# Dense blocks of 128 rows instead of 256 in a fused top-k attention and squared-ReLU network

## The chip, the cores and the metric

The kernel runs on one core of a Trainium2 chip. The metric is the device time of one execution in microseconds (us); lower is better. The core's engines work side by side, each through its own list of instructions in order: TensorE (PE; its weight loads are PEld), VectorE (DVE), ScalarE (ACT), GpSimd (POOL), and SyncE (SP), which here issues the DMAs.

## The reference

For 8 batches and 8 heads of 576 queries and keys of 64 numbers, each query keeps its 32 highest scores; the softmax runs over these alone. The result, 4608 tokens of 512 numbers, goes through a dense network of width 2048.

```python
scores = scale * np.matmul(q, k.transpose(0, 1, 3, 2))
kth = np.partition(scores, -top_k, axis=-1)[..., -top_k:-top_k + 1]
scores = np.where(scores >= kth, scores, -1000000000.0)
scores = scores - np.max(scores, axis=-1, keepdims=True)
attn = np.exp(scores)
attn = attn / (np.sum(attn, axis=-1, keepdims=True) + 1e-09)
x = np.matmul(attn, v)            # as [4608, 512] tokens
...
h = np.maximum(x @ w_in, 0.0)     # w_in 512 x 2048
out = h * h @ w_out               # w_out 2048 x 512
```

## The kernel before

**Steps.** The attention runs in 144 steps, counted by `u` from 0. A step takes two groups of 128 query rows (two heads of one chunk; a batch has four chunks of 128 rows and a rest of 64). The steps are software-pipelined: while step u finds the top 32 of its rows, PE computes the scores of step u + 3 (`scores`, L213) and ACT copies them out of the accumulation banks (L219); DVE prepares step u + 2 (`split`, L251 or L253 to L256, and `join`, L263); ACT and POOL make the weights of step u - 1 (`below` L354, `expo` L363, `mask` L359); SP turns them by a DMA transpose (`turn`, L402); PE multiplies them with the values (`products`, L429); and ACT puts the divided result into a chunk of tokens, `x_tok` (`place`, L457). Steps 0 to 124 are one loop (L702), 125 to 141 a second one (L798), in which the dense work that is left is taken faster; the last two are written out.

**Top 32.** Per step DVE does four rounds of MAX8 (L302) with three MATCH_REPLACE8 between them (L306), on candidates that `split` and `join` have sorted: maxima and minima of the halves and quarters of a row. The minima are POOL's: it adds (L278) and subtracts the maxima (L270) as whole numbers.

**Who takes the maxima.** `split` has two ways. It "lends" when POOL has room: one DVE operation of 576 columns (L251), and `bring` (L235), a PE product with the unit matrix, hands a part of the result back into the bank that `join` reads. Otherwise DVE does three operations of 288 columns (L253, L254, L256) and POOL gets less. A step that lends may also be "joint": then `join` does one operation of 288 columns on DVE (L263) and POOL one more (L270 of 288), otherwise DVE does two. `bring` waits for ACT's copies of the next scores, and `join` waits for `bring`.

**The ledger.** The order is fixed when the program is written. `debt` counts the work owed by POOL ("G") and ACT ("A"); each step takes off 5.76 and 6.0, and `owe` adds what is issued. `split` lends outside the last steps only while the debt of POOL is under 4.9 (L239), and is joint while it is under 3.68 at first, from step 125 on 4.28.

**Dense work.** When a chunk of `x_tok` is full, `x_unit` (L474) turns it by DMA (L497) into `xT`. After the second chunk of a pair, and three steps later (two near the end), `block` (L519) opens a block of 256 rows. It has 8 "ups" and 8 "downs". An up is a piece for PE: two of the 16 slices of w_in, each with 4 matmuls of 256 columns (L531), into a bank of 512 columns. ACT takes the ReLU of it (L537), and the square is ACT's (L542) or POOL's (L545), by the ledger; up to step 18 and in the last ones it is always POOL's. A down is 4 matmuls with w_out (L559); after four downs ACT copies the rows out (L566) and SP stores them. The rests of 64 rows of two batches, and the last batch's chunks, make blocks of 128 rows already, with 4 ups of 4 slices. `dense` (L591) gives PE two pieces a step, an up and a down in turn if both are there, in the loop's two places, before `bring` and at the step's end; without work it issues idle matmuls (`idle_piece`, L575).

**Buffers.** `h2` holds the hidden rows, 3 buffers of 256 rows; the raw weights land in the same buffers (`weight_units`, L606), 16 loads from step 1 on, one a step, and 16 casts by ACT or POOL from step 4 on, one a step (L785).

Of the kernel before, what the change touches and what calls it, by code (L numbers as in the profile page):

```python
# [14 lines left out]
bf16 = mybir.dt.bfloat16  # L15
# [7 lines left out]
def kernel(  # L23
# [10 lines left out]
    B, H, S, D = q.shape  # L34
# [8 lines left out]
    KH, NF = 4, d_ff // 128  # L43
# [12 lines left out]
    now = [0]  # L56
# [139 lines left out]
    Z, DEEP = U - 19, 9  # L196
# [271 lines left out]

    moves, ups, downs = [], [], []
    ripe = {}  # L470
    xts = {}


    def x_unit(now, b, c):  # L474
        last = b == B - 1
        cs = (c,) if last else (c - c % 2, c - c % 2 + 1)
        if c == cs[0]:
            xts[b, cs] = ffp.tile([128, len(cs), KH, 128], bf16, name=f"xT_{len(cs)}", bufs=2)
        xt = xts[b, cs]
        to = xt[:, c - cs[0]]  # L480

        def done():
            if c == cs[-1]:
                stores = [[(slice(0, 128), out[b * S:b * S + 512].rearrange("(p c) d -> p c d", c=4)[:, z])] for z in cs]
                block(lambda kh: xt[:, :, kh, :], stores)

        def by_tensor(now):
            tp = ps_one.tile([128, KH, 128], bf16, name="gen", bufs=2)
            for kh in range(KH):
                pin(nc.tensor.transpose(tp[:, kh, :], x_tok[b, c][:, kh * 128:(kh + 1) * 128], id_h[:, :]))  # L490
            pin(nc.scalar.activation(to, tp[:, :, :], AF.Copy))
            done()

        if last:
            moves.append(by_tensor)
        else:
            pin(nc.sync.dma_start_transpose(out=to, in_=x_tok[b, c][:, :]))  # L497
            ripe.setdefault(now + (3 if now < Z - 8 else 2), []).append(done)

    def rem_unit(now, b):  # L500
        owe(A=0.3)
# [17 lines left out]
    def block(xt, stores):  # L519
# [4 lines left out]
        def up(f0):  # L524
            def go():
                if f0 == 0:
                    held["h2"] = ffp.tile([128, NF, 256], bf16, name="h2", bufs=3)
                hp = ps_one.tile([128, 512], f32, name="gen", bufs=2)[:, :]
                for n in range(per):
                    for kh in range(KH):  # L530
                        pin(nc.tensor.matmul(out=hp[:, n * n_rows:(n + 1) * n_rows], lhsT=w_in[:, kh, (f0 + n) * 128:(f0 + n + 1) * 128],  # L531
                                             rhs=xt(kh), start=(kh == 0), stop=(kh == KH - 1)))
                h2 = held["h2"][:, f0:f0 + per, 0:n_rows]

                def bend():
                    rl = ffp.tile([128, 512], f32, name="rl", bufs=4)
                    pin(nc.scalar.activation(rl[:, :], hp, AF.Relu))  # L537
                    owe(A=0.5)
                    flat = rl[:, :].rearrange("p (n r) -> p n r", n=per)
                    if DEEP + 9 < now[0] < U - 7 and debt["A"] < 6.0 and debt["G"] > 3.6:  # L540
                        owe(A=0.62)
                        later.append(lambda: pin(nc.scalar.activation(h2, flat, AF.Square)))  # L542
                        return
                    owe(G=1.05)
                    squares.append(lambda by: pin(by.tensor_mul(h2, flat, flat)))  # L545
                    if not hold["squares"]:
                        square()
                late.append(bend)
                if f0 + per == NF:
                    downs.extend(down(c, p) for c in range(len(stores)) for p in range(4))  # L550
            return go
# [54 lines left out]
    def weight_units():  # L606
        loads, casts = [], []
        for dst, src in ((w_in, moe_w_in.rearrange("(kh p) n -> p kh n", p=128)), (w_out, moe_w_out.rearrange("(kh p) n -> p kh n", p=128))):
            to, width = dst[:, :, :], src.shape[2]
            for g in range(8):  # L610
                if width >= 1024:
                    at = (slice(None), g // 2, slice((g % 2) * 1024, (g % 2) * 1024 + 1024))
                else:
                    at = (slice(None), slice(2 * g, 2 * g + 2), slice(None))
                box = {}

                def load(src=src, at=at, box=box):
                    t = ffp.tile([128, NF, 256], bf16, name="h2", bufs=3)
                    t = t[:, :, :].rearrange("p f r -> p (f r)")[:, 0:2048].bitcast(f32)
                    box["t"] = t if not isinstance(at[1], slice) else t.rearrange("p (a n) -> p a n", a=2)  # L620
                    pin(nc.sync.dma_start(out=box["t"], in_=src[at]))

                def cast(dst=dst, at=at, box=box):
                    if debt["A"] > debt["G"]:
                        owe(G=1.25)
                        pin(nc.gpsimd.tensor_copy(dst[at], box["t"]))
                    else:
                        owe(A=0.95)
                        pin(nc.scalar.activation(dst[at], box["t"], AF.Copy))
                loads.append(load)  # L630
                casts.append(cast)
# [70 lines left out]
    for u in range(Z):  # L702
# [79 lines left out]
        if 1 < u < 24 and not ups and not downs:  # L782
            idle_piece(2)
        turn_x(u)
        if w_casts and u >= 4:  # L785
            w_casts.pop(0)()
        if w_loads and u >= 1:
            w_loads.pop(0)()
# [75 lines left out]
    u = U - 2  # L864
# [36 lines left out]
        square()  # L901
    empty(two)

    xl = ffp.tile([128, KH, 128], bf16, name="xT_1", bufs=2)
    hl = ffp.tile([128, NF, 256], bf16, name="h2", bufs=3)

    def x_last(khs):
        tp = ps_one.tile([128, KH, 128], bf16, name="gen", bufs=2)
# [219 lines left out]
```

## Time and profile before

| | before |
|---|---|
| median of 3 runs | 843.42 us (843.41 to 844.8) |
| the profiled execution | 843.64 us |
| its span, first to last instruction | 841.8 us |
| DVE busy | 816.4 us, 97% |
| ACT busy | 791.5 us, 94% |
| POOL busy | 785.0 us, 93% |
| PE busy, matmuls | 710.4 us, 84% |
| chain that ended last | DVE 53%, issue 15%, POOL 13%, ACT 11%, PE 7% |

The busy times are unions of the instructions' times on one engine; the chain goes back from the last instruction to what released each. A step takes some 5.4 to 5.5 us. All numbers of the trace are of this one execution, so a sum is made against 843.64 us.

### The profile page before, as it was taken

Reading aid. Unit: us, or ns where it says so; the run is one execution under the profiler, and the core shown is the slowest. Engines: PE = TensorE matmul, PEld = TensorE weight load, DVE = VectorE, ACT = ScalarE, POOL = GpSimd, SP = SyncE. Lnnn points to the kernel's source line nnn. Section 1 sums busy time; section 2 is a strip of 40 time slices with the busy share of each in tenths; the row PEclk is TensorE's granted clock in tenths of the full one; section 3 lists DMA queues with packets and bytes.
Section 4 is the critical chain, followed back from the end, with each engine's and each line's share of the span. In section 5 each row is a group of like instructions: output and inputs, shape, how many; then the busy total and the mean of one; then the engine's idle time right before and its main releaser. Section 6 shows DMA issues by size and latency. Waiting matters only on the chain.

```text
span 841.8 us, 19913 instructions
## 1 busy us (share of the span) xinstructions
PE 710.4 (84%) x6061; PEld 446.6 (53%) x6062; DVE 816.4 (97%) x3411; ACT 791.5 (94%) x1513; POOL 785.0 (93%) x638
## 2 busy tenths in 40 slices
PE   8898987788888879788788888788888888989986
PEld 4554545455545545455555554455555554656554
DVE  5999999999999999999999999999999999999995
ACT  4897999999999999999999999999999999999983
POOL 3788999999999999999999999999999999999771
PEclk9999999999999999999999999999999999999999
DMA  4796786654546556445565455555566557433442
GB/s 112 163 216 158 193 178 112 111 118 101 118 105 104 117 111 130 97 103 109 114 124 110 104 111 124 124 111 109 118 104 124 118 104 152 79 76 64 94 84 55
DMA packets 300883, 98.06 MB, mean 116 GB/s; under 512 B 284768, under 2 KB 293216, under 8 KB 300768
## 3 DMA queue, kind: packets, MB, share of 16 engines
q1 hardware_dynamic: 299424, 96.28, 56.1%
q8 instruction: 50, 0.82, 0.4%
q14 instruction: 65, 0.53, 0.2%
q10 hardware_dynamic: 1344, 0.43, 0.2%
HBM read 36.70 MB, written 9.44 MB: 55 GB/s over the span
## 4 chain that ended last, share of the span: by engine, by line
DVE 53%; issue 15%; POOL 13%; ACT 11%; PE 7%; DVEq 0%; ACTq 0%; POOLq 0%
DVE m L302 23%; DVE cat L306 15%; DVE s L251 7%; POOL cat L270 7%; DVE cat L263 5%; POOL cat L278 5%; ACT s L219 3%; ACT h L542 2%; PE sc_b L235 2%; ACT rl L537 1%; ACT marks_b L354 1%; ACT marks_a L354 1%; ACT w_two_a L363 1%; PE sc_b L213 1%; PE dn_ps L578 1%
## 5 line engine op out<-in xcount | busy, mean ns | idle before, releaser
L302 DVE MAX8 m<-cat 128x8 f32<-128x100 f32 (+3 forms) x1152 | 428.7, 414 | 0.2
L278 POOL TENSOR_TENSOR cat<-s 128x864 int32<-128x864 int32 (+2 forms) x144 | 265.0, 1840 | 5.9 <-DVE cat L263 3.5
L306 DVE MATCH_REPLACE8 cat<-m,cat 128x100 f32<-128x100 f32 (+2 forms) x864 | 252.7, 300 | 0.1
L270 POOL TENSOR_TENSOR cat<-cat,s 128x576 int32<-128x576 int32 (+1 forms) x144 | 196.3, 1363 | 3.3 <-DVE s L251 1.8
L213 PE MATMUL sc_b<-qkT 64*128 64x288 f32 (+1 forms) x640 | 117.4, 447 | 55.3 <-DVE cat L263 49.2
L235 PE MATMUL sc_b<-s,id_f 128*128 128x144 f32 x536 | 98.3, 306 | 57.4 <-ACT s L219 56.5
L559 PE MATMUL dn_ps<-w_out,h 128*128 128x512 bf16 x560 | 143.9, 382 | 1.3 <-POOL h L545 0.7
L531 PE MATMUL gen<-xT,w_in 128*128 128x256 bf16 (+1 forms) x1088 | 128.6, 263 | 1.9 <-ACT rl L537 1.1
L235 PEld LDWEIGHTS sc_b<-s,id_f 128*128 128x128 f32 x536 | 75.0, 190 | 101.0 <-ACT s L219 97.4
L531 PEld LDWEIGHTS <-w_in 128*128 128x128 bf16 x1344 | 110.2, 98 | 32.3 <-issue 19.7
L354 ACT ACTIVATE marks_a<-s,m 128x576 bf16<-128x576 f32 x144 | 124.2, 871 | 0.4 <-POOL w_two_c L359 0.2
L354 ACT ACTIVATE marks_b<-s,m 128x576 bf16<-128x576 f32 x142 | 118.5, 847 | 0.0
L219 ACT ACTIVATE s<-sc_b 128x576 f32<-128x576 f32 x144 | 103.7, 720 | 15.5 <-PE sc_b L213 8.2
L213 PE MATMUL sc_a<-qkT 64*128 64x288 f32 (+1 forms) x640 | 111.5, 430 | 0.4 <-DVE s L251 0.3
L219 ACT ACTIVATE s<-sc_a 128x576 f32<-128x576 f32 x144 | 104.8, 728 | 5.5 <-PE sc_a L213 3.7
L251 DVE TENSOR_TENSOR s<-sc_a,s 128x576 f32<-128x576 f32 x134 | 100.2, 748 | 0.0
L537 ACT ACTIVATE rl<-gen 128x512 f32<-128x512 f32 x140 | 96.3, 692 | 0.5 <-PE gen L531 0.5
L213 PEld LDWEIGHTS sc_b<-qkT 64*128 64x128 f32 (+1 forms) x640 | 47.6, 175 | 85.5 <-DVE cat L263 64.9
L270 POOL TENSOR_TENSOR cat<-cat 128x288 int32<-128x288 int32 x113 | 89.2, 789 | 0.9 <-DVE shares L434 0.9
L542 ACT ACTIVATE h<-rl 128x512 bf16<-128x512 f32 x123 | 89.2, 729 | 0.0
L559 PEld LDWEIGHTS <-h 128*128 128x128 bf16 x560 | 47.8, 98 | 68.4 <-issue 31.9
L263 DVE TENSOR_TENSOR cat<-sc_b,s 128x288 f32<-128x288 f32 x175 | 75.0, 444 | 5.8 <-PE sc_b L235 5.8
(137 smaller groups left out, 1190.5 us busy)
## 6 DMA issues: line engine op xcount, KB each, us to landing
v_raw<-in_v_dram SPq DMA_DIRECT2D x31, 256.0 KB, 3.1
out_dram<-wide SPq DMA_DIRECT2D x31, 256.0 KB, 2.9
q_raw<-in_q_dram SPq DMA_DIRECT2D x30, 256.0 KB, 3.6
k_raw<-in_k_dram SPq DMA_DIRECT2D x30, 256.0 KB, 3.6
h<-in_moe_w_in_dram SPq DMA_DIRECT2D x8, 512.0 KB, 5.1
h<-in_moe_w_out_dram SPq DMA_DIRECT2D x8, 512.0 KB, 4.7
q_raw<-in_q_dram SPq DMA_DIRECT2D x32, 32.0 KB, 3.1
v_raw<-in_v_dram SPq DMA_DIRECT2D x32, 32.0 KB, 2.7
```

The lines of the kernel that those rows point to most:

```text
L213: pin(nc.tensor.matmul(out=sc[j][r if rest else slice(0, 128), x, 0:HALF], lhsT=qkT[r, 0, c * 128:min(S, (c + 1) * 128)], rhs=qkT[r, 1, j ...
L219: pin(nc.scalar.activation(s[:, :, j, :], sc[j][:, :, 0:HALF], AF.Copy))
L235: pin(nc.tensor.matmul(out=far[:, x, :], lhsT=id_f[:, :], rhs=st[w]["tops"][:, x, 1, :], start=True, stop=True))
L251: pin(tt(tops, *quarters, op=ALU.max))
L263: pin(nc.vector.tensor_tensor(d["cat"][:, :, lo:lo + QUAR], far, d["tops"][:, :, 0, :], op=op))
L270: pin(nc.gpsimd.tensor_tensor(at, at, top, op=ALU.subtract))
L278: pin(nc.gpsimd.tensor_tensor(cat[:, :, QUAR + lo:QUAR + hi], both[:, :, 0, lo:hi], both[:, :, 1, lo:hi], op=ALU.add))
L302: pin(nc.vector.max(out=m[r][:, x, :], in_=cat[:, x, at]))
L306: pin(nc.vector.match_replace(out=cat[:, x, at], in_to_replace=m[r][:, x, :], in_values=cat[:, x, at], imm_value=NEG))
L354: pin(nc.scalar.activation(pairwise(marks[u % 2][:, x, :]), d["s"][:, x], AF.Relu, bias=d["m"][3][:, x, 7:8], scale=-1.0))
L531: pin(nc.tensor.matmul(out=hp[:, n * n_rows:(n + 1) * n_rows], lhsT=w_in[:, kh, (f0 + n) * 128:(f0 + n + 1) * 128], rhs=xt(kh), start=(kh ...
L559: pin(nc.tensor.matmul(out=op[:, :], lhsT=held["h2"][:, f, c * 128:(c + 1) * 128], rhs=w_out[:, f, :], start=(f == 0), stop=(f == NF - 1)))
```

## The change

Every chunk that is turned gets a block of its own, of 128 rows: 28 blocks of 4 ups and 4 downs in place of 14 of 8 and 8. An up of such a block has 4 slices with 4 matmuls of 128 columns. `h2` becomes 5 buffers of 128 rows, `xT` 4 buffers of one chunk. Up to step 20 a block opens two steps after its turn, not three, and the casts of the weights start in step 3.

```diff
--- before.py
+++ after.py
@@ -468,21 +468,14 @@
 
     moves, ups, downs = [], [], []
     ripe = {}
-    xts = {}
 
 
     def x_unit(now, b, c):
         last = b == B - 1
-        cs = (c,) if last else (c - c % 2, c - c % 2 + 1)
-        if c == cs[0]:
-            xts[b, cs] = ffp.tile([128, len(cs), KH, 128], bf16, name=f"xT_{len(cs)}", bufs=2)
-        xt = xts[b, cs]
-        to = xt[:, c - cs[0]]
+        to = ffp.tile([128, KH, 128], bf16, name="xT", bufs=4)
 
         def done():
-            if c == cs[-1]:
-                stores = [[(slice(0, 128), out[b * S:b * S + 512].rearrange("(p c) d -> p c d", c=4)[:, z])] for z in cs]
-                block(lambda kh: xt[:, :, kh, :], stores)
+            block(lambda kh: to[:, kh, :], [[(slice(0, 128), out[b * S:b * S + 512].rearrange("(p c) d -> p c d", c=4)[:, c])]])
 
         def by_tensor(now):
             tp = ps_one.tile([128, KH, 128], bf16, name="gen", bufs=2)
@@ -495,7 +488,7 @@
             moves.append(by_tensor)
         else:
             pin(nc.sync.dma_start_transpose(out=to, in_=x_tok[b, c][:, :]))
-            ripe.setdefault(now + (3 if now < Z - 8 else 2), []).append(done)
+            ripe.setdefault(now + (3 if 20 < now < Z - 8 else 2), []).append(done)
 
     def rem_unit(now, b):
         owe(A=0.3)
@@ -524,7 +517,7 @@
         def up(f0):
             def go():
                 if f0 == 0:
-                    held["h2"] = ffp.tile([128, NF, 256], bf16, name="h2", bufs=3)
+                    held["h2"] = ffp.tile([128, NF, 128], bf16, name="h2", bufs=5)
                 hp = ps_one.tile([128, 512], f32, name="gen", bufs=2)[:, :]
                 for n in range(per):
                     for kh in range(KH):
@@ -615,7 +608,7 @@
                 box = {}
 
                 def load(src=src, at=at, box=box):
-                    t = ffp.tile([128, NF, 256], bf16, name="h2", bufs=3)
+                    t = ffp.tile([128, NF, 128], bf16, name="h2", bufs=5)
                     t = t[:, :, :].rearrange("p f r -> p (f r)")[:, 0:2048].bitcast(f32)
                     box["t"] = t if not isinstance(at[1], slice) else t.rearrange("p (a n) -> p a n", a=2)
                     pin(nc.sync.dma_start(out=box["t"], in_=src[at]))
@@ -782,7 +775,7 @@
         if 1 < u < 24 and not ups and not downs:
             idle_piece(2)
         turn_x(u)
-        if w_casts and u >= 4:
+        if w_casts and u >= 3:
             w_casts.pop(0)()
         if w_loads and u >= 1:
             w_loads.pop(0)()
@@ -901,8 +894,8 @@
         square()
     empty(two)
 
-    xl = ffp.tile([128, KH, 128], bf16, name="xT_1", bufs=2)
-    hl = ffp.tile([128, NF, 256], bf16, name="h2", bufs=3)
+    xl = ffp.tile([128, KH, 128], bf16, name="xT", bufs=4)
+    hl = ffp.tile([128, NF, 128], bf16, name="h2", bufs=5)
 
     def x_last(khs):
         tp = ps_one.tile([128, KH, 128], bf16, name="gen", bufs=2)
```

The ledger sees the blocks at other times, so the order of the program moves. The first place is DVE where step 15 begins: the last join of step 14 (L263), then the split for step 17, and the first round of step 15. Before:

```order
L263 TENSOR_TENSOR cat<-sc_b,s 128x2x144
L251 TENSOR_TENSOR s<-sc_a,s 128x4x144
L302 MAX m<-cat 128x8 x2
L306 MATCH_REPLACE cat<-m,cat 128x100 x2
L440 RECIPROCAL shares<-av_ps 128x4
```

and with the change:

```order
L263 TENSOR_TENSOR cat<-sc_b,s 128x2x144
L253 TENSOR_TENSOR sc_b<-sc_a,s 128x2x144
L254 TENSOR_TENSOR s<-sc_a,s 128x2x144
L256 TENSOR_TENSOR cat<-sc_a,s 128x2x144
L302 MAX m<-cat 128x8 x2
L306 MATCH_REPLACE cat<-m,cat 128x100 x2
L440 RECIPROCAL shares<-av_ps 128x4
```

Step 15 no longer lends: three operations stand for one, and at its end two joins for one. Over the program that is 133 steps with L251 in place of 134, 11 with L253 to L256 in place of 10, and 176 joins in place of 175. Which steps are joint also shifts (15, 16, 17, 19 and 21 are not, before 20 to 23).

The second place is ACT in step 124, between the copies of the scores of this step and of the next (`rl` is a ReLU's result, `h2` a square, `w_two` the exponentials, `marks` the masks, `qkT` a head's turned queries). Before:

```order
L457 ACTIVATE x_tok_8932<-av_ps_121,shares_120 128x64 x2
L354 ACTIVATE marks_b_118<-s_9400,m_8449 128x576
L345 ACTIVATE low_9740<-neg_9738 128x1
L363 ACTIVATE w_two_a_103<-s_9400,low_9666 128x2x576
L363 ACTIVATE w_two_b_104<-s_9482,low_9740 128x2x576
L146 ACTIVATE qkT_9701<-gen_9772 128x512
L354 ACTIVATE marks_a_117<-s_9482,m_8449 128x576 x2
L457 ACTIVATE x_tok_9009<-av_ps_121,shares_120 128x64 x4
```

and with the change (L530 is the ReLU, L535 the square there):

```order
L457 ACTIVATE x_tok_9656<-av_ps_121,shares_120 128x64 x2
L354 ACTIVATE marks_b_118<-s_10177,m_9117 128x576
L345 ACTIVATE low_10546<-neg_10544 128x1
L530 ACTIVATE rl_10555<-gen_10520 128x512
L363 ACTIVATE w_two_a_103<-s_10177,low_10448 128x2x576
L535 ACTIVATE h2_10378<-rl_10555 128x512
L363 ACTIVATE w_two_b_104<-s_10266,low_10546 128x2x576
L530 ACTIVATE rl_10590<-gen_10572 128x512
L146 ACTIVATE qkT_10495<-gen_10597 128x512
L354 ACTIVATE marks_a_117<-s_10266,m_9117 128x576
L535 ACTIVATE h2_10378<-rl_10590 128x512
```

Two ReLUs and two squares have come into this step. In steps 119 to 121 ACT gets one ReLU and one square less, in steps 125 to 135 two ReLUs less; from the copies of step 119 to those of step 136 it is the same number of ReLUs (24) and output copies (6), and 21 squares for 20. Over the whole program ACT has the same number of each, and the squares on POOL stay 17, six of them now before step 24 in place of three. Idle matmuls of 512 columns on `dn_ps` go from 203 to 165. SP's DMAs keep their number and kinds.

## Rows read from the trace of the kernel before

**Rows 1.** Busy time by stretch, 200 to 700 us (stretch, length, busy us of each engine, instructions).

```profile
200.00:700.00 500.00, 417.21 (x3592) 266.64 (x3590) 497.40 (x2084) 493.03 (x947) 500.00 (x385) 1.00 0.56 114
```

**Rows 2.** DVE's waits, first from 80 to 718 us, then from 718 to 786.

```profile
DVE cat L306 <- POOL cat L270: 1.1, 5, 0.3
DVE cat L263 <- PE sc_b L235: 0.8, 3, 0.4
...
DVE cat L263 <- PE sc_b L235: 4.0, 6, 1.1
```

**Rows 3.** PE's waits from 718 to 786 us.

```profile
PE sc_b L235 <- ACT s L219: 3.7, 5, 1.4
```

**Rows 4.** Busy time by stretch: step 14, steps 126 to 136, steps 137 to 141.

```profile
95.17:100.58 5.41, 5.23 (x38) 2.73 (x36) 5.41 (x24) 5.41 (x10) 5.41 (x5) 1.00 0.77 208
...
718.35:785.10 66.75, 61.13 (x579) 41.26 (x580) 62.60 (x269) 66.75 (x137) 65.48 (x52) 1.00 0.39 75
785.10:816.03 30.93, 26.71 (x250) 15.66 (x248) 30.75 (x133) 27.39 (x55) 21.09 (x22) 1.00 0.44 91
```

**Rows 5.** Pieces on PE in order of time (start, us); then the loads of w_in.

```profile
764.47 1.05 PE L531 MATMUL gen<-xT,w_in 128*128 128x256 bf16 x8
765.35 1.03 PE L559 MATMUL dn_ps<-w_out,h 128*128 128x512 bf16 x4
...
771.00 1.06 PE L531 MATMUL gen<-xT,w_in 128*128 128x128 bf16 x16
771.90 1.03 PE L559 MATMUL dn_ps<-w_out,h 128*128 128x512 bf16 x4
...
L531 PEld LDWEIGHTS <-w_in 128*128 128x128 bf16 x1344 | 110.2, 98 | 32.3 <-issue 19.7 <-PE sc_b L213 0.4
```

**Rows 6.** DVE's groups, shapes apart (busy us, mean ns of one).

```profile
L251 DVE TENSOR_TENSOR s<-sc_a,s 128x576 f32<-128x576 f32 x134 | 100.2, 748 | 0.0
...
L253 DVE TENSOR_TENSOR sc_b<-sc_a,s 128x288 f32<-128x288 f32 x10 | 4.7, 465 | 2.0 <-ACT s L219 1.6
...
L256 DVE TENSOR_TENSOR cat<-sc_a,s 128x288 f32<-128x288 f32 x10 | 4.5, 448 | 0.0
```

**Rows 7.** POOL's groups, shapes apart.

```profile
L278 POOL TENSOR_TENSOR cat<-s 128x864 int32<-128x864 int32 x113 | 227.6, 2014 | 0.0
L270 POOL TENSOR_TENSOR cat<-cat,s 128x576 int32<-128x576 int32 x134 | 188.3, 1405 | 2.6 <-DVE s L251 1.8
L270 POOL TENSOR_TENSOR cat<-cat 128x288 int32<-128x288 int32 x113 | 89.2, 789 | 0.9 <-DVE shares L434 0.9
...
L545 POOL TENSOR_TENSOR h<-rl 128x512 bf16<-128x512 f32 x17 | 17.6, 1044 | 0.2 <-ACT rl L537 0.2
L278 POOL TENSOR_TENSOR cat<-s 128x288 int32<-128x288 int32 x10 | 7.9, 794 | 5.9 <-DVE cat L263 3.5 <-ACT s L219 2.4
```

**Rows 8.** SP's first chunk turn; DMA issues with us to landing.

```profile
92.21 1.38 SPq L497 DMA_TRANSPOSE xT<-x_tok  x1
...
h<-in_moe_w_in_dram SPq DMA_DIRECT2D x8, 512.0 KB, 5.1
...
xT<-x_tok SPq DMA_TRANSPOSE x28, 2.7
```

**Rows 9.** ACT in order of time in steps 126 and 127 (start, us).

```profile
723.86 0.66 ACT L537 ACTIVATE rl<-gen 128x512 f32<-128x512 f32 x1
724.34 0.85 ACT L354 ACTIVATE marks_a<-s,m 128x576 bf16<-128x576 f32 x1
725.00 0.70 ACT L542 ACTIVATE h<-rl 128x512 bf16<-128x512 f32 x1
725.52 0.84 ACT L354 ACTIVATE marks_a<-s,m 128x576 bf16<-128x576 f32 x1
```

**Rows 10.** Busy time by stretch, 68 to 74 us; PE's granted clock stands third from the right.

```profile
68.00:70.00 2.00, 0.25 (x2) 0.25 (x4) 2.00 (x5) 0.47 (x1) 1.46 (x2) 1.00 1.10 358
...
72.00:74.00 2.00, 1.94 (x7) 1.02 (x7) 1.00 (x4) 2.00 (x4) 2.00 (x2) 0.51 0.42 79
```

## The prediction

> **What bounds the kernel now.** I read the busy time by stretches first, since an average over the program hides which engine ends the waits where. From 200 to 700 us VectorE (DVE) is busy 497.4 of 500 us, GpSimd (POOL) all 500.0, ScalarE (ACT) 493.0 and TensorE (PE) 417.2 [rows 1]. The reader is to see three engines with next to no idle time. In that part a change can only add or take work on DVE or POOL; a better order of dense pieces on PE has no idle time of DVE to win back.
>
> Next come DVE's own waits. From 80 to 718 us it waits 1.1 us on POOL's second halves (L270) and 0.8 us on `bring`, the PE product that hands the borrowed maxima back (L235) [rows 2]. From 718 to 786 us it waits 4.0 us, in six waits, always on `bring` [rows 2]. Who makes `bring` late stands in PE's waits of that stretch: 3.7 us on ACT's copies of the scores (L219) [rows 3]. And the stretch 718.35 to 785.10 (steps 126 to 136) shows why: ACT is busy 66.75 of 66.75 us while DVE reaches 62.60 [rows 4]. So the last part before the end is bound by ACT, the long middle by DVE and POOL together. After 785.10 DVE is busy 30.75 of 30.93 us, ACT has 3.5 us and POOL 9.8 us to spare [rows 4].
>
> **The change, part by part.** The sum is made against the profiled execution: 843.64 us, 841.8 of it span, 1.84 around it. That is 0.22 above the median of the three runs shown, 843.42. A measurement of this kernel tells about 0.2% from no change, 1.7 us.
>
> *TensorE.* 14 blocks of 256 rows become 28 of 128. Relus, squares, output copies and down products keep their number; only the up products are cut otherwise: a piece of 8 matmuls of 256 columns becomes one of 16 of 128. The kernel before has both. The piece of eight starts at 764.47 and the next piece 0.88 us later; the piece of sixteen starts at 771.00 and its successor 0.90 us later [rows 5]. 112 pieces at 0.02 make 2.2 us of PE, spread over 128 steps, and 38 idle matmuls fewer take more than that away. PE has 83 us free between 200 and 700 [rows 1]. Cost 0; without that cover it would be 2.2 us.
>
> *DVE in step 15.* The first block now starts in step 14 and not 19. Its four squares are sent to POOL, which in the program's ledger pushes POOL's debt over the limit when step 15 splits its scores. So one step no longer borrows POOL: three operations of 288 columns (465, 448 and 448 ns) take the place of one of 576 (748), and one more join is done, of the shape that takes 448 [rows 6]: 1.36 - 0.75 + 0.45 = 1.06 us. DVE has no idle time there: in the window that starts with step 14 it is busy 5.41 of 5.41 us [rows 4]. This term is the surest of all, +1.06.
>
> *POOL in the same steps.* Three squares more at 1044 ns, +3.13. The step that doesn't borrow, and doesn't join on POOL, swaps 2014 + 1405 + 789 for twice 794 (the two kinds of 288 columns cost the same), -2.62 [rows 7]. Net +0.51. POOL has no gap from 200 to 700, and DVE's waits on it (1.1 us) show that it sets the pace by the end of the middle [rows 1, 2]. Where POOL sets the pace, DVE's 1.06 us come out of DVE's waits and only POOL's 0.51 stay; where it doesn't, 1.06 stay. I take 0.8 for both terms together.
>
> *Weight loads and chunk turns.* Five landing buffers for three, casts a step sooner. A load now has two steps, some 11 us, before its cast; w_in takes 5.1 us to land [rows 8]. Loads, turns and casts keep their number and their order on SP. Nothing, then; were the cover gone, a cast would hold ACT or POOL for the rest of a landing, at most 5.1 us once. The early chunks get two steps, not three, from turn to use: the first turn is issued at 92.21 and lands some 2.7 us later, 94.9, and step 14, which uses it, begins at 95.17 [rows 4, 8]. The cover is thin but there; if a turn came 1 us late, PE would stand 1 us before `bring`. The four buffers for the turned chunks hold as much as two pairs did, and five hidden blocks of 128 rows are more than the two or three that are open at once.
>
> *ACT in the middle.* Before, two chunks arrive at once, so some steps have two ups and some none; now most have one. The bursts make ACT's copies late, which is the 0.8 us wait on `bring` [rows 2]. I take half of it back: -0.4, with 0 and -0.8 as bounds.
>
> *ACT in the tail.* Here the order of work decides. Between the score copies of step 124 and of step 125 ACT gets two relus and two squares that were not there. From one start to the next a relu takes 0.48 and a square 0.52 us [rows 9]: 2.0 us more. In the three steps before, it gets one relu and one square less, 1.0 us. From step 125 to 136 two relus fewer, -0.96. Over the whole stretch, from the copies of step 119 to those of step 136, that is one square more, +0.52. ACT is the bound, so lateness there is DVE's wait. If the lead of 1.0 us is lost because ACT catches up with DVE in between, the peak is +2.0. If smoother steps let every copy come in time, the waits of 4.0 us go. I take +0.5, nearest to the count, with -4.0 and +2.0 as ends. After step 136 four ups fall into one step, where ACT has room [rows 4]: 0.
>
> Sum: 843.64 + 0.8 - 0.4 + 0.5 = 844.54 for a profiled execution, 844.3 against the median; I say **844.4 us**.
>
> **Rivals.** *Slower: ACT's backlog is carried to the end.* Place: step 124, with two ups where there were none. Price: the whole 2.0 us in the tail, 1.06 in the head, nothing back in the middle: 843.6 + 3.1 = 846.7. For it: ACT has no gap from 718 to 785, so nothing is recovered there. Against: its work in these steps is nearly the same in total. It decides if ACT is already level with DVE when step 124 begins.
>
> *Faster: even steps end the waits of the tail.* The 4.0 us on `bring` and the 0.8 go, 1.06 is paid: 843.6 - 3.7 = 839.9. For it: all these waits follow steps with two or three ups. Against: the tail has just as many relus, and 100% of ACT is not a burst.
>
> *PE's clock falls in sparse steps.* Steps 16, 17 and 29 to 31 have one piece and two idle matmuls now. PE is busy 0.25 of the two us before 70; from 72 to 74 the granted clock is 0.51, the lower of its two levels, 1.2 GHz, and DVE stands still 1.0 us of the two [rows 10]. Two such places: 843.6 + 0.8 + 2 = 846.4. Against: from 80 to 718 us DVE waits on `bring` only three times [rows 2], so it mostly comes early enough to be slowed a little.
>
> *The narrow pieces are bound by their weight loads.* A load of w_in has a mean of 98 ns [rows 5]. If a 128-column matmul had to wait for its whole load, a piece of sixteen would take 1.57 us, 0.69 more than the 0.88. Some 16 pieces in steps 126 to 136 would add 11 us to a PE that has 5.6 free there [rows 4], so DVE would be 5.4 later: some 849. Against it: the piece of sixteen that did take 0.90 [rows 5], 56 ns a matmul, so loads run under the matmuls. The Trainium skill (TensorE: Matmul & The Clock Gate, section "Back-to-back issue gap") says that a real stream of load and matmul keeps about 81 ns a matmul at 128 columns; by that a piece would take an estimated 1.30 us, 0.42 more, and the sum 1.1 us more in the tail, where 16 such pieces ask 6.7 us. The trace, with 56, doesn't agree, and I go by it.
>
> **How the numbers follow.** Forecast 0.58, with its own range 842.6 to 845.6; backlog 0.17; smooth tail 0.15; clock 0.06; weight loads 0.04. The range that holds 8 in 10 takes in the forecast's, the clock's and the nearer half of the two large cases: 841.6 to 846.6. Faster by over 0.2% (below 841.7) is the smooth tail alone, 0.15. Slower (above 845.1) is backlog, clock and weight loads, 0.27, and the upper edge of the forecast, 0.03: 0.30. Within 0.2%: 0.55.
>
> **What would show it.** Right: DVE has 11 triples of L253, L254 and L256 and 133 of L251; pieces of sixteen start 0.9 us before their successors; DVE's waits on `bring` from step 126 to 136 come to 4 to 5 us with ACT at 100%; the waits on POOL in the middle shrink. Wrong: those tail waits under 2 us or over 6; a wait of DVE or PE on `xT` or on a square in steps 14 to 20; a granted clock under 1 in a stretch where `bring` has no slack; PE waits on w_out.

## The result and the profile after

| | before | after |
|---|---|---|
| median | 843.41 us (843.21 to 844.8, 4 runs) | 853.0 us (852.39 to 854.2, 4 runs) |
| ratio, 95% interval | | 1.0111 (1.0098 to 1.0123) |
| span of the profiled execution | 841.8 us | 850.8 us |

The change is 9 us slower, outside the range of 841.6 to 846.6. The page of the kernel after has these lines:

```profile
PE 702.2 (83%) x6831; PEld 462.6 (54%) x6920; DVE 817.1 (96%) x3414; ACT 791.8 (93%) x1513; POOL 782.8 (92%) x637
...
DVE  5999999999999999999999999999999997999985
...
PEclk9999999999999999999999999999999998999998
```

DVE is busy 0.7 us longer in a span that is 9.0 longer; only the weight loads, which overlap the matmuls, grew (PEld 462.6 us, before 446.6). So DVE waits more, and the slices say where: near the end, where its 7 and PE's clock of 8 stand.

To find the steps, each step's length is counted from DVE's first maximum over 100 elements to the next step's. The stretches of steps 122, 123, 125, 126 to 136, 140 and the last one, 143, in the kernel after (stretch, length, busy us of PE, PEld, DVE, ACT and POOL with instructions, PE's granted clock, DMA share, GB/s):

```profile
695.60:701.99 6.39, 1.93 (x12) 0.68 (x10) 6.29 (x27) 4.53 (x9) 6.39 (x6) 0.82 0.87 172
701.99:709.89 7.90, 7.46 (x73) 6.25 (x74) 5.98 (x26) 5.10 (x11) 5.33 (x7) 0.71 0.61 120
...
715.32:723.85 8.53, 5.41 (x49) 3.42 (x48) 6.05 (x28) 8.50 (x18) 8.08 (x8) 1.00 0.28 56
723.85:790.24 66.39, 61.73 (x676) 42.66 (x684) 62.66 (x268) 66.39 (x136) 63.19 (x49) 1.00 0.41 76
809.51:818.60 9.09, 6.81 (x49) 3.24 (x49) 6.57 (x29) 5.61 (x11) 5.58 (x7) 1.00 0.28 68
828.25:850.85 22.60, 14.27 (x165) 10.53 (x164) 12.75 (x43) 9.72 (x23) 4.48 (x7) 0.90 0.19 49
```

The same view of the kernel before, steps 123, 125, 140 and 143 (126 to 136 stand in [rows 4]):

```profile
701.16:707.06 5.90, 4.89 (x36) 2.49 (x34) 5.90 (x26) 5.87 (x13) 5.65 (x7) 1.00 0.68 156
712.48:718.35 5.87, 4.26 (x32) 2.02 (x28) 5.87 (x28) 5.66 (x15) 5.87 (x6) 1.00 0.40 78
804.37:810.84 6.47, 5.79 (x36) 2.47 (x34) 6.37 (x28) 6.30 (x12) 5.20 (x6) 1.00 0.48 75
820.50:841.82 21.32, 13.10 (x157) 9.72 (x154) 12.59 (x43) 8.54 (x20) 4.12 (x6) 0.92 0.24 54
```

Three steps carry most of it: step 123 is 2.0 us longer, 125 2.7, 140 2.6; the last is 1.3 longer. Up to step 122 the kernel after is 0.8 later, 0.57 of that before the first step is reached; steps 126 to 136 are 0.4 shorter. DVE is busy at most 0.2 us longer in each of the three steps, so nearly all of this is DVE waiting. Its waits, first in steps 121 to 126 (where before it has none), then 127 to 136, then 137 to 142 (from L474 on, line numbers are 7 lower after):

```profile
DVE cat L263 <- PE sc_b L235: 2.0, 1, 2.0
DVE shares L440 <- ACT rl L530: 1.9, 1, 1.9
DVE shares L440 <- PE av_ps L429: 0.5, 1, 0.5
...
DVE cat L263 <- PE sc_b L235: 3.6, 7, 0.9
...
DVE shares L434 <- PE av_ps L429: 2.1, 1, 2.1
```

The second line names ACT for the wait on L440, but L440 reads the products of PE. PE's waits in steps 121 to 126, then in 137 to 142, show what it stood behind:

```profile
PE sc_b L235 <- ACT s L219: 4.9, 3, 3.1
PE gen L524 <- DMA xT<-x_tok: 4.7, 1, 4.7
...
PE dn_ps L571 <- ACT wide L559: 1.4, 1, 1.4
```

Three causes are argued for here and called A, B and D; the letters C, E and F of the expectations stand for rivals that are told there.

**A, the late chunk.** For 4.7 us PE stands in front of the first up of a block, and everything queued behind that up stands too. SP's queue and PE's in order of time (start, us; in brackets the idle time before, and what ended it):

```profile
694.49 1.36 SPq L402 DMA_TRANSPOSE wT<-w_two_c  x1
695.90 0.72 SPq L125 DMA_DIRECT2D q_raw<-in_q_dram  x1
...
698.50 0.62 SPq L126 DMA_DIRECT2D k_raw<-in_k_dram  x1
699.19 1.26 SPq L490 DMA_TRANSPOSE xT<-x_tok  x1
...
702.27 1.89 PE L524 MATMUL gen<-xT,w_in 128*128 128x128 bf16 x16 [4.75 <-DMA xT<-x_tok]
```

The chunk is turned at the end of step 120, and near the end a block opens two steps later, in 122. On SP its turn stands behind the turn of the weights, which waits for POOL's mask until 694.49, and behind four loads, whose issues take 0.6 to 0.7 us each: it is issued at 699.19, 3.6 us into step 122. Before, the same chunk waited for its partner, and the pair opened in step 126. While PE stands its clock falls, and stays down for the first up, which takes 1.89 us, where [rows 5] have 1.06. The same columns as above, from 698 to 706 us:

```profile
698.00:700.00 2.00, 0.00 (x0) 0.00 (x0) 2.00 (x7) 2.00 (x4) 2.00 (x3) 0.94 0.89 197
700.00:702.00 2.00, 0.00 (x0) 0.00 (x0) 1.90 (x7) 0.13 (x1) 2.00 (x3) 0.50 0.83 143
702.00:704.00 2.00, 1.73 (x17) 1.73 (x18) 0.90 (x7) 0.00 (x0) 2.00 (x3) 0.50 0.78 146
704.00:706.00 2.00, 2.00 (x20) 1.91 (x19) 1.18 (x9) 1.45 (x3) 1.25 (x3) 0.50 0.57 69
```

The Trainium skill (TensorE: Matmul & The Clock Gate, section "Part 1: The HAM clock gate") has it that an idle array gets 1.2 GHz, half of the full clock; the trace agrees, with 0.50 from 700 to 702 us, where PE does nothing.

**B, ACT's burst.** In step 125 ACT is busy 8.50 of 8.53 us. Between its score copies at 712.45 and at 721.01 stand two relus (L530) and two squares (L535) that the kernel before has not there:

```profile
712.45 0.69 ACT L219 ACTIVATE s<-sc_a 128x576 f32<-128x576 f32 x1
...
714.13 0.66 ACT L530 ACTIVATE rl<-gen 128x512 f32<-128x512 f32 x1
...
715.75 0.70 ACT L535 ACTIVATE h<-rl 128x512 bf16<-128x512 f32 x1
...
717.42 0.66 ACT L530 ACTIVATE rl<-gen 128x512 f32<-128x512 f32 x1
...
719.04 0.71 ACT L535 ACTIVATE h<-rl 128x512 bf16<-128x512 f32 x1
...
721.01 0.76 ACT L219 ACTIVATE s<-sc_b 128x576 f32<-128x576 f32 x1
```

So 8.6 us lie between these copies, and the second begins 5.69 us into step 125. In the kernel before it is 6.6 us, and 2.21 us into the step:

```profile
708.12 0.66 ACT L219 ACTIVATE s<-sc_a 128x576 f32<-128x576 f32 x1
...
714.69 0.71 ACT L219 ACTIVATE s<-sc_b 128x576 f32<-128x576 f32 x1
```

**D, idle pieces on the down bank.** In step 140 the queue is empty (before it still held six downs), and an idle piece, the matmuls that keep PE busy, is put in its place. It writes the one bank of the downs, and so waits until ACT has copied the last output out; the products of step 140 wait behind it. PE in order of time:

```profile
811.33 0.65 PE L213 MATMUL sc_a<-qkT 64*128 64x288 f32 x4
813.36 1.02 PE L571 MATMUL dn_ps<-fill,id_h 128*128 128x512 bf16 x4 [1.38 <-ACT wide L559]
814.23 0.47 PE L429 MATMUL av_ps<-vau_a,wT 128*128 128x65 bf16 x10
```

### The profile page after: what moved, and what is told of

Read it like the earlier page. It is cut to its first block, busy times and chain, and to the rows that moved or that the text cites. A ratio compares the mean times of both kernels' runs of the same rounds, so it can differ in the third digit from the quotient of the medians.

```text
span 850.8 us, 21500 instructions
## 1 busy us (share of the span) xinstructions
PE 702.2 (83%) x6831; PEld 462.6 (54%) x6920; DVE 817.1 (96%) x3414; ACT 791.8 (93%) x1513; POOL 782.8 (92%) x637
## 4 chain that ended last, share of the span: by engine, by line
DVE 49%; issue 16%; POOL 16%; PE 10%; ACT 8%; SPq 0%; DMA 0%; POOLq 0%; DVEq 0%; ACTq 0%
DVE m L302 22%; DVE cat L306 14%; POOL cat L278 7%; POOL cat L270 7%; DVE s L251 6%; DVE cat L263 5%; ACT s L219 2%; PE gen L524 2%; PE sc_b L213 2%; PE dn_ps L552 1%; PE sc_b L235 1%; ACT rl L530 1%; PE dn_ps L571 1%; ACT h L535 1%; PE sc_a L213 1%
## 5 line engine op out<-in xcount | busy, mean ns | idle before, releaser
L278 POOL TENSOR_TENSOR cat<-s 128x864 int32<-128x864 int32 (+2 forms) x144 | 270.1, 1875 | 9.6 <-DVE cat L263 3.7
L270 POOL TENSOR_TENSOR cat<-cat,s 128x576 int32<-128x576 int32 (+1 forms) x144 | 201.7, 1401 | 3.0 <-DVE s L251 1.5
L524 PEld LDWEIGHTS <-w_in 128*128 128x128 bf16 x2240 | 132.8, 99 | 38.8 <-issue 28.7
L524 PE MATMUL gen<-xT,w_in 128*128 128x128 bf16 x1984 | 134.0, 222 | 6.5 <-DMA xT<-x_tok 4.7
L552 PE MATMUL dn_ps<-w_out,h 128*128 128x512 bf16 x486 | 130.4, 383 | 7.8 <-issue 4.0
L354 ACT ACTIVATE marks_a<-s,m 128x576 bf16<-128x576 f32 x144 | 123.3, 862 | 0.9 <-DVE m L302 0.6
L213 PE MATMUL sc_a<-qkT 64*128 64x288 f32 (+1 forms) x640 | 113.3, 438 | 0.0
L530 ACT ACTIVATE rl<-gen 128x512 f32<-128x512 f32 x140 | 95.2, 683 | 6.6 <-PE gen L524 6.6
L251 DVE TENSOR_TENSOR s<-sc_a,s 128x576 f32<-128x576 f32 x133 | 99.1, 745 | 0.0
L270 POOL TENSOR_TENSOR cat<-cat 128x288 int32<-128x288 int32 x112 | 94.3, 842 | 2.6 <-DVE shares L434 2.5
L535 ACT ACTIVATE h<-rl 128x512 bf16<-128x512 f32 x123 | 89.2, 727 | 0.0
L263 DVE TENSOR_TENSOR cat<-sc_b,s 128x288 f32<-128x288 f32 x176 | 75.1, 442 | 6.4 <-PE sc_b L235 6.3
```

The source lines that it names most:

```text
L213: pin(nc.tensor.matmul(out=sc[j][r if rest else slice(0, 128), x, 0:HALF], lhsT=qkT[r, 0, c * 128:min(S, (c + 1) * 128)], rhs=qkT[r, 1, j ...
L251: pin(tt(tops, *quarters, op=ALU.max))
L263: pin(nc.vector.tensor_tensor(d["cat"][:, :, lo:lo + QUAR], far, d["tops"][:, :, 0, :], op=op))
L270: pin(nc.gpsimd.tensor_tensor(at, at, top, op=ALU.subtract))
L278: pin(nc.gpsimd.tensor_tensor(cat[:, :, QUAR + lo:QUAR + hi], both[:, :, 0, lo:hi], both[:, :, 1, lo:hi], op=ALU.add))
L354: pin(nc.scalar.activation(pairwise(marks[u % 2][:, x, :]), d["s"][:, x], AF.Relu, bias=d["m"][3][:, x, 7:8], scale=-1.0))
```

## The experiments

A table first. With the same code ahead of it, the first step begins up to 0.9 us sooner or later from one profiled execution to the next, and that has nothing to do with these steps, so the table has the time from the start of step 121 to the end of step 140, and DVE's idle time in it, from the profiled execution of each run. After, idle_gen and warm run the same program up to step 136, and their idle time in steps 123, 125 and 126 is 4.4, 4.9 and 5.5 us together: so a difference of 1 us there, between two single executions, can be chance. Each ratio is against runs of the kernel before that were taken with it, and their median went from 843.41 to 844.77; medians of two rows are not to be subtracted.

| run | steps 121 to 140 | 123 | 125 and 126 | 127 to 136 | 140 | median, us | ratio to before (95%) |
|---|---|---|---|---|---|---|---|
| before | 122.2 | 0 | 0 | 4.2 | 0.1 | 843.41 | |
| after | 129.2 | 1.9 | 2.5 | 3.7 | 2.5 | 853.0 | 1.0111 (1.0098 to 1.0123) |
| late_open | 128.8 | 0 | 4.1 | 4.1 | 2.1 | 851.25 | 1.008 (1.0062 to 1.0097) |
| turn_first | 126.9 | 0 | 2.1 | 4.1 | 2.1 | 849.56 | 1.0064 (1.0042 to 1.0086) |
| up_sooner | 126.3 | 0 | 0.9 | 4.9 | 2.1 | 848.98 | 1.006 (1.0044 to 1.0077) |
| pool_squares | 126.0 | 0 | 1.0 | 4.1 | 2.1 | 848.15 | 1.005 (1.0033 to 1.0067) |
| idle_gen | 128.2 | 1.7 | 3.2 | 4.1 | 0.7 | 850.45 | 1.0081 (1.0057 to 1.0105) |
| warm | 130.4 | 2.0 | 3.5 | 4.1 | 2.1 | 852.65 | 1.01 (1.0083 to 1.0117) |
| old_open | 131.0 | 1.4 | 4.7 | 4.1 | 2.1 | 851.68 | 1.009 (1.0073 to 1.0107) |
| mended | 126.5 | 0 | 1.9 | 5.3 | 0.7 | 847.43 | 1.0044 (1.0031 to 1.0057) |
| pairs | 124.5 | 0 | 1.9 | 4.3 | 0.1 | 845.79 | 1.0019 (1.0008 to 1.003) |
| pairs_gen | 123.3 | 0 | 0.4 | 4.6 | 0.1 | 843.55 | 1.0003 (0.9994 to 1.0011) |
| before_gen | 122.6 | 0 | 0 | 4.5 | 0.1 | 844.86 | 1.0014 (1.0005 to 1.0023) |
| spare | 122.8 | 0 | 0.5 | 3.9 | 0.1 | 844.06 | 0.9994 (0.9983 to 1.0004) |

**late_open: the block of step 122 opens in 123.**

```diff
-            ripe.setdefault(now + (3 if 20 < now < Z - 8 else 2), []).append(done)
+            ripe.setdefault(now + (3 if 20 < now < Z - 4 else 2), []).append(done)
```

> One number of the change is altered: near the end a turned chunk is opened three steps after its turn up to step 120, not only up to 116. By the planner's order that moves one block, from step 122 to step 123, and nothing else. Theory A (the late chunk: PE stands in front of the first up in step 122 because the turn is still queued on SP, and DVE's waits of steps 123 and 125 follow from it): PE's wait on the turned chunk (4.7 us) is gone, DVE's waits of 1.9 us in step 123 and 2.5 us in step 125 with it, time 853.0 - 4.4 = 848.6. Theory B (ACT's burst of two relus in step 124, the rival of the prediction): the wait in step 125 stays near 2 us, time 851. Theory C (PE's clock fell because the pieces are sparse): the clock still falls in steps 121 to 123, and 2 us or more stay.

Measured: PE's wait on the turned chunk is gone and step 123 takes 5.90 us again, but steps 125 and 126 lose 4.1. So A is right for step 123 and wrong for 125: that wait needs no stop of PE two steps earlier. Theory B keeps it, and the later block makes it longer. PE then stands 3.1 us behind ACT's copies, its clock is 0.50 from 720 to 725.5, and the two downs there make the next scores late: the clock lengthens a stall, it doesn't begin it. The `bring` of step 125 takes 1.33 us there, in the kernel after 0.76:

```profile
719.30 1.33 PE L235 MATMUL sc_b<-s,id_f 128*128 128x144 f32 x4 [3.12 <-ACT s L219]
```


**turn_first: the chunk's turn ahead of the weights' turn on SP.**

```diff
             mask(u - 1)
+            if u >= Z - 8:
+                turn_x(u)
             turn(u - 1)
```

> From step 117 on, the full chunk is turned before the step's weights are turned, not after them, so that on SP its turn stands ahead of the one that waits for POOL's mask. The block still opens in step 122, as in the change. Theory A (the transfer is late since it stands behind a waiting turn): the transfer lands before step 122 opens it, PE's wait of 4.7 us is gone or under 1 us, time 848.6 to 849.5. If instead opening a block in step 122 is itself the fault (too much work for PE or ACT there), the waits of steps 123 and 125 stay, time 852 to 853. Theory B: the wait in step 125 stays, 851. Risk: the turn now waits for the last copy of the chunk by ACT, and the weights' turn behind it may come late by as much; then products are late and DVE waits on shares.

Measured: the turn is issued at 690.70, 3.8 us before step 122 begins, where the kernel after issues it 3.6 us into the step: 7.4 us sooner. SP's queue:

```profile
690.70 1.26 SPq L490 DMA_TRANSPOSE xT<-x_tok  x1
693.41 1.35 SPq L402 DMA_TRANSPOSE wT<-w_two_c  x1
```

The block still opens in step 122, and step 123 has no wait. So it was the transfer's place in the queue that cost these 2 us. The wait in step 125 stays, 1.7 us, as B says; the clock of 0.75 in step 123 costs DVE nothing there. The copies and the `bring` of step 125, which begins at 712.25:

```profile
716.61 0.75 ACT L219 ACTIVATE s<-sc_b 128x576 f32<-128x576 f32 x1
717.42 1.22 PE L235 MATMUL sc_b<-s,id_f 128*128 128x144 f32 x4 [3.12 <-ACT s L219]
```

So the copies begin 4.36 us into the step, 2.15 later than before, and `bring` takes another 0.5 us longer than at the full clock.

**up_sooner and pool_squares: two ways to take work off ACT in step 124**, both on top of turn_first. The first takes one up in step 123, the second gives the squares of step 124 to POOL.

```diff
-        for n in range(2 if len(ups) + len(downs) > 24 or (x == 1 and u >= 100 and u % 3 == 0 and len(ups) + len(downs) > 4) else 1):
+        for n in range(2 if len(ups) + len(downs) > 24 or (x == 1 and u >= 100 and u % 3 == 0 and len(ups) + len(downs) > (2 if u == Z - 2 else 4)) else 1):
```

```diff
-                    if DEEP + 9 < now[0] < U - 7 and debt["A"] < 6.0 and debt["G"] > 3.6:
+                    if DEEP + 9 < now[0] < U - 7 and now[0] != Z - 1 and debt["A"] < 6.0 and debt["G"] > 3.6:
```

> On top of the run with the turn moved ahead on SP, one up piece (one relu and one square) is taken in step 123, where ACT is idle for 1.0 us, and not in step 124, so that step 124 has one relu and not two. Theory B (ACT's burst of two relus and two squares in step 124 makes the copies of the next scores late, and DVE waits on bring in step 125; the late chunk only adds to it): DVE's waits on bring in steps 125 and 126, 1.7 and 0.4 us in that run, fall to under 1.0 us together, time 849.6 - 1.2 = 848.4. Theory A alone (all of it came from the late chunk): nothing left to gain there, 849.6. In both, the wait of 1.7 us in step 140 stays.

> On top of the run with the turn moved ahead on SP, the two squares of step 124 are made by POOL and not by ACT. Theory B: ACT is done 1.04 us sooner before the copies of step 125, DVE's wait there falls from 1.7 to 0.7 us and that of step 126 goes; POOL's ledger makes step 125 do one join more on DVE, 0.45 us: 849.6 - 1.0 - 0.4 + 0.4 = 848.6. If the copies are late because DVE or PE was late and ACT only follows: the wait stays at 1.7, time 850.0.

Measured: 2.1 us in steps 125 and 126 become 0.9 and 1.0. The copies and the `bring` of step 125, of up_sooner (the step begins at 713.32) and then of pool_squares (712.94):

```profile
717.41 0.71 ACT L219 ACTIVATE s<-sc_b 128x576 f32<-128x576 f32 x1
718.17 0.76 PE L235 MATMUL sc_b<-s,id_f 128*128 128x144 f32 x4 [2.15 <-ACT s L219]
```

```profile
716.25 0.74 ACT L219 ACTIVATE s<-sc_b 128x576 f32<-128x576 f32 x1
717.04 0.76 PE L235 MATMUL sc_b<-s,id_f 128*128 128x144 f32 x4 [2.08 <-ACT s L219]
```

In pool_squares the copies begin 3.31 us into the step, 1.05 sooner than in turn_first, as two squares less on ACT should make it: this bears B out. In up_sooner they begin only 0.3 sooner, and the other 0.5 is `bring` at the full clock, so that run says less. The medians don't tell these three runs apart, and each gain rests on one execution. Part of it isn't won for good: up_sooner loses 0.8 again in steps 127 to 136, where ACT is idle for only 0.2 us, and pool_squares pays one more join on DVE and waits 0.9 in step 126.

**idle_gen: the idle pieces of the last loop on a bank of the ups.**

The edit stands at both places of that loop.

```diff
-            idle_piece()
+            idle_piece(4, "gen", 2)
```

> In the loop of the last steps the idle piece goes to one of the two banks of the up pieces and not to the one bank of the down pieces, which ACT has to copy out first. Theory D (with blocks of 128 rows the queue runs empty right behind a last down piece, so that the idle piece stops PE until ACT's copy of the output is done, and the products behind it are late): the wait of 1.4 us in front of the idle piece in step 140 is gone, DVE's wait there is 2.1 - 1.4 = 0.7 us, time 853.0 - 1.4 = 851.6. Rival (the bunch of four ups and four downs in steps 138 and 139 makes the scores late, whatever the idle piece does): DVE's wait in step 140 stays at 2.1 us, time 853.0.

Measured: 0.7 us of idle time in step 140 in place of 2.5, and the step takes 7.23 us, not 9.09. The idle piece follows the scores at once:

```profile
811.15 0.65 PE L213 MATMUL sc_a<-qkT 64*128 64x288 f32 x4
811.73 1.04 PE L571 MATMUL gen<-fill,id_h 128*128 128x512 bf16 x4
812.61 0.47 PE L429 MATMUL av_ps<-vau_a,wT 128*128 128x65 bf16 x10
```

D holds, for 1.4 to 1.9 us: the runs that leave the idle pieces where they are wait 2.1 to 2.5. The 0.7 us that remain stand before the products, which follow late scores (four ups and four downs begin in steps 138 and 139) and the idle piece; which of the two makes them was not tried.

**warm: fourteen empty matmuls in place of six before the last two steps** (`empty(one, 7)` for `empty(one, 3)`).

> Fourteen matmuls that add zeros to a free bank, in place of six, before the last two steps. Theory E (PE's clock falls to its lower level in the last steps because PE stands idle for 2 us before them, and the ups run slowly there, 1.3 us longer in step 143): the granted clock stays at 1.0 there, step 143 takes 21.3 us and not 22.6, time 851.7. If the step is longer because work arrives late and not because the clock is low: clock 1.0 but the same 22.6 us, time 853.0.

Measured: step 143 takes 21.48 us at a mean clock of 0.94, so the clock did not stay at 1.0. But late_open, without them, takes 21.42 at 0.90, and over all runs but the kernel after the step takes 20.75 to 22.13. So most of the 1.3 us of the last step is within what executions differ by; that the clock makes them is not shown.

**old_open: three steps from turn to use in the early part, as before.**

```diff
-            ripe.setdefault(now + (3 if 20 < now < Z - 8 else 2), []).append(done)
+            ripe.setdefault(now + (3 if now < Z - 8 else 2), []).append(done)
```

> Only the early part is put back: a chunk turned before step 21 waits three steps, as in the kernel before, and not two. The first block then opens in step 15. The step that does not borrow POOL is 16, not 15, so its 1.06 us of DVE stay; steps 14 to 20 have one or two pieces a step, not a block at once. If the head costs by the early opening, the sum of the lengths of steps 14 to 29, 0.5 us above before in the change, falls to about 0.2; the time is 853.0 - 0.3 = 852.7, and steps 122 to 143 are as in the change.

Measured: steps 14 to 29 take 89.35 us, against 89.92 after and 89.44 before. The early opening costs 0.6, a little more than expected.

**pairs: blocks of 128 rows, opened two at a time.** Narrow pieces, buffers and casts are those of the change.

```diff
         def done():
-            block(lambda kh: to[:, kh, :], [[(slice(0, 128), out[b * S:b * S + 512].rearrange("(p c) d -> p c d", c=4)[:, c])]])
+            opened.append(lambda: block(lambda kh: to[:, kh, :], [[(slice(0, 128), out[b * S:b * S + 512].rearrange("(p c) d -> p c d", c=4)[:, c])]]))
+            if last or len(opened) == 2:
+                while opened:
+                    opened.pop(0)()
```

> The change with its blocks of 128 rows and all its buffers, but a block is opened only when the second chunk of a pair is there, and then both at once, as in the kernel before. No block opens in step 122, and the queue does not run empty in steps 137 to 140. Theories A, B and D (what costs is when the blocks open: late chunk, burst in step 124, idle pieces in step 140): PE's wait on a turned chunk, DVE's 2 us waits in steps 123, 125 and 140 are all gone, time 843.9 plus or minus 0.8. Theory F (narrow up pieces cost by themselves, or the smaller buffers or the earlier casts do): 846 or more, spread over the steps.

Measured: steps 123 and 140 are as before, and 2 us stay in step 125. There the queue is empty, and PE's waits name D again:

```profile
PE dn_ps L575 <- ACT wide L563: 2.4, 1, 2.4
```

**pairs_gen: the same with the idle pieces off the down bank; before_gen: that move alone in the kernel before; mended: single blocks with turn_first, up_sooner, idle_gen and old_open together.**

> The run with blocks opened in pairs, and the idle pieces of the last loop moved off the bank of the down pieces. Theory D for step 125 of that run (its queue is empty there, so an idle piece stands 2.4 us behind ACT's copy of an output, and DVE waits 1.9 us on bring behind it): DVE's wait in step 125 is gone, time 845.8 - 1.9 = 843.9, no more than the kernel before. Rival (PE's lower clock in 716 to 720 us makes bring late): the wait shrinks by half at most, 845.

> Control: the kernel before with the same move of the idle pieces. There one idle piece stands in that loop, in step 125, and DVE does not wait behind it. Theory D says the bank costs only where the queue runs empty right behind a last down piece: no difference, 844.0 within 0.5. If the bank of the idle pieces matters by itself: 1 us less or more.

> The change with its single blocks kept, and the four mends that did something put together: the turn ahead on SP from step 117 on, one up in step 123 in place of 124, idle pieces off the down bank, and three steps from turn to use in the early part too. If the causes are separate and add up: 853.0 - 2.0 (step 123) - 2.0 (steps 125 and 126) + 0.6 (what that run lost again in steps 128 to 135) - 1.4 (step 140) - 0.6 (head) - 1.0 (last steps) = 846.6, still above the kernel before by 2 to 3 us. If smaller buffers, casts or narrow pieces cost something spread out, 849 or more.

Measured: pairs_gen takes 843.55 us, 1.0003 (0.9994 to 1.0011) of before. Its steps 125 and 140:

```profile
712.34:718.72 6.38, 5.40 (x48) 3.33 (x46) 5.99 (x28) 5.73 (x14) 6.38 (x6) 1.00 0.37 72
805.33:811.81 6.48, 5.74 (x51) 3.15 (x49) 6.38 (x29) 6.18 (x12) 5.21 (x6) 1.00 0.45 85
```

So rows of 128, smaller buffers and earlier casts cost nothing together that the medians show; the 9 us go with when the blocks open and with the bank of the idle pieces. The ledger blurs this a little: DVE has two joins fewer in pairs_gen than before, its steps 14 to 29 are 0.5 us shorter, and its steps 121 to 140 are 1.1 longer. The control missed: 844.86, 1.2 us slower by the ratio, of which its profiled execution, 842.86, shows 0.4 in steps 121 to 140. So the move is no gain in itself. Mended gives 847.43, 0.8 above what was expected: the causes add up nearly, and single blocks still cost 3.7 us by the ratio. In its one execution steps 125 and 126 wait 1.9, 127 to 136 1.2 more than before, and step 140 0.6. The gain of up_sooner in step 125 is not seen again: the copies begin 4.73 us into the step. So for single blocks no edit here takes B away whole; opening in pairs does.

**spare: pairs_gen with one square each of steps 133 and 134 on POOL.**

```diff
+                    if now[0] in spare:
+                        spare.remove(now[0])
-                    if DEEP + 9 < now[0] < U - 7 and debt["A"] < 6.0 and debt["G"] > 3.6:
+                    elif DEEP + 9 < now[0] < U - 7 and debt["A"] < 6.0 and debt["G"] > 3.6:
```

> A try at beating both kernels: the pairs with their idle pieces off the down bank, and one square each of steps 133 and 134 is made by POOL, which stands idle 1.1 and 0.9 us there, and not by ACT, which is busy all of the time while DVE waits 1.0 and 0.8 us on bring. If ACT's work is what bring waits for: 0.5 us less in each of two steps, 843.5 - 1.0 = 842.5. If POOL's square of 1.05 us makes POOL's own second halves late: a wait on POOL takes its place, 843.5 or a little more.

Measured: 844.06 us, 0.9994 (0.9983 to 1.0004): not told apart from the kernel before. Step 135 waits 0.5 us less, 133 and 134, which were forecast to lose 0.5 each, the same. No version here beats both kernels.

## Why the prediction was wrong, by its own steps

*TensorE: right.* A piece of sixteen starts at 726.08 and its successor 0.90 us later, as in [rows 5]; with 112 narrow pieces pairs_gen is no slower than the kernel before. The rival of weight loads falls. The Trainium skill (TensorE: Matmul & The Clock Gate, section "Back-to-back issue gap") has about 81 ns a matmul for such a stream; the trace doesn't agree, with 0.90/16, 56 ns.

```profile
726.08 1.07 PE L524 MATMUL gen<-xT,w_in 128*128 128x128 bf16 x16
726.98 0.34 PE L235 MATMUL sc_b<-s,id_f 128*128 128x144 f32 x1
```

*DVE and POOL in the first steps: right in kind, somewhat too dear.* DVE has 11 triples and 133 of L251, as forecast. I said +0.8; steps 14 to 29 are 0.5 longer, since steps 20 to 23 get shorter by 1.2 together, and old_open gives 0.6 back.

*The middle: half a microsecond too hopeful.* The waits on `bring` from 80 us to step 121 are gone, but those on POOL grow from 1.1 us [rows 2] to 2.4 by step 120, where I said they would shrink; steps 30 to 120 take 504.1 us, before 504.0. So nothing of the 0.4 came back.

*"Weight loads and chunk turns ... Nothing, then": the first step that failed.* I looked at the early turns, whose cover I called thin, and they did hold: no wait on `xT` there. The late ones, by the same rule of two steps, I didn't cost at all. The first block that opens alone near the end meets a turn that stands on SP behind another turn, which waits for POOL, and behind four loads: 2.0 us.

*"ACT in the tail": the peak of 2.0 was right, the value of +0.5 the second step that failed.* The two relus and two squares in step 124 were counted and priced at 2.0, and my reason for taking +0.5 was a lead of 1.0 us from the steps before, kept until step 124. It was not kept. In the kernel after ACT stood idle for 1.9 and 2.8 us in steps 122 and 123, waiting for PE. In turn_first, where PE doesn't stop, the copies begin 1.10 us into step 122, against 2.97 before, but 0.69 into step 124, against 0.53: ACT was idle for 0.6 and 1.0 us in between, and the lead was gone. The wait is 2.1 us there, 2.5 in the kernel after. The rival "ACT's backlog is carried to the end", 846.7 at 0.17, was this part of the truth. The waits from 126 to 136, forecast at 4 to 5 us, came to 3.7.

*"After step 136 four ups fall into one step, where ACT has room: 0": the third step that failed.* ACT had room; PE's order was the matter. I counted ACT's work and didn't ask what PE does when the queue is empty: 2.4 us in step 140, of which another bank for the idle pieces takes away up to 1.9.

*The clock: the rival's condition came, its price did not.* The clock fell in two of the places that it named, in steps 16 and 17 and in step 31, and DVE stayed busy for all of the time (same columns as above):

```profile
114.00:116.00 2.00, 2.00 (x8) 0.44 (x5) 2.00 (x14) 1.74 (x5) 2.00 (x3) 0.50 0.74 258
...
191.00:193.00 2.00, 1.67 (x6) 0.60 (x8) 2.00 (x15) 1.66 (x5) 2.00 (x2) 0.54 0.00 0
```

So the 2 us of that rival are 0. Near the end the clock fell after PE had been stopped by A, and there it made the stall longer; turn_first has 0.75 in step 123 with no wait of DVE.

All in all, 0.6 before the first step, 0.2 to step 121, 2.0, 2.7, -0.4, 2.6 and 1.3 in the last step make the 9.0 us of the span. Open are the last step's 1.3 and the 0.6 at the start, which executions of other runs have in part and in part not; and why steps 73 to 79 are 1.1 to 1.2 us longer in the trace of every version of the change but old_open, where it is 0.6, was not tried; in the kernel after DVE waits 0.9 us on POOL in them.

## What to carry to other kernels

Smaller units change when work opens, and the cost sits there, not in the unit: ask of every unit what its transfer is queued behind when it opens alone, and what the engines do in the step in which the queue now runs empty. A filler must not write a bank that another engine has yet to empty, where work that the bounding engine needs stands behind it. A lead that one engine is to keep over another is worth nothing in a sum until a row shows that it is kept.

## What was not expected of the hardware

A stop of PE can cost twice: after 4.7 us without work the clock stayed at 0.50 from 700 to 706 us, and the next up took 1.89 us. But a low clock alone cost nothing in steps 17 and 31, where DVE was busy throughout. And a turn that SP issues behind one that waits, and behind four loads, came 7.4 us later in its step than the same turn ahead of them, though it depends on nothing of theirs.
